# Memory attention and a bilinear FFN on one core: the maximum over tokens is spread by transposition and DRAM transfers, the first w_out block is converted whole, and the engines' orders are written anew

## The chip, the core and the metric

The kernel runs on one core of a Trainium2 chip. A core has five instruction streams: TensorE (PE in the profile; its weight loads are PEld), VectorE (DVE), ScalarE (ACT), GpSimd (POOL) and SyncE (SP), which issues the DMAs. The metric is the time of one execution on the device in microseconds; the runs of the kernel before took 499.88 us in the median.

## The reference, cut to what matters

Eight batches, eight heads, 576 tokens, head dimension 64, 32 memories for each head:

```python
a = phi - np.max(phi, axis=2, keepdims=True)          # over the 576 tokens
a = np.exp(a)
a = a / (np.sum(a, axis=2, keepdims=True) + 1e-09)
k_m = np.einsum('bhsm,bhsd->bhmd', a, k)
v_m = np.einsum('bhsm,bhsd->bhmd', a, v)
scores = matmul(q, k_m^T) / sqrt(64)                  # softmax over the 32 memories
x = softmax(scores) @ v_m                             # -> (4608, 512)
...
a = x @ w1
b = x @ w2
return (a * b @ w3) @ w_out                           # 512x1024, 512x1024, 1024x1024, 1024x512
```

The four weights come as 64-bit words and are turned into fp32 on the chip.

## The kernel before, in words

**What is computed where.** The product w3 @ w_out doesn't depend on the tokens, so the kernel forms it once (`product`, L607) and then needs only one matrix multiplication behind a*b. Its first half (list token W0k, with X for block k = 0) uses w3's columns of one half, the second half (W1k) those of the other; k counts 8 blocks of 128 rows. Each weight block is loaded by SP (`fetch`, L523) and converted in five stages C1 to C5 on ScalarE and VectorE, one stage of one task at a time. Attention works with phi in two layouts: `ph` (memories on the partitions, tokens along the free axis; for the maximum and the sum over tokens) and `a` (tokens on the partitions; for the products with k and v). The maximum is found in `ph` by VectorE (`top`, L212: one value for each of 128 partitions and two halves), but it must be subtracted in `a`, where the memories run along the free axis: every partition needs all 256 values. `spread_max` (token `bm`, L230) makes them with two TensorE transpositions of a broadcast column into a PSUM bank, and `sub_max` (token `bs`, L236 and L240) adds that bank to `a`; `exp_tok` (`be`, L244, ScalarE) follows, then `memories` (`mem`, L252 and L261), which multiplies `a` with the k and v rows (tiles kv0, kv2 and kv4, loaded at L181 and L188, and the chunk in kv2 used first), `blocks` (L283), and `scores` (L301, with `q`). `tokens_down` (L316) turns the scores so that VectorE can do the softmax (L328 to L344).

**The FFN part.** For each batch of 576 tokens the products with the folded weights are done as fp32 pairs of high and low parts (h and l tokens, L497 and L814) in a scheme of seven block products (P{i}{q}, L744, six records each; then O{i}{part}, L829, twelve records each). M tokens (L416) are the products of the next batch's memories with w1 and w2. In the first batch A tokens (L714) stand in for P.

**What sets the order.** Four lists of tokens, written by hand, give the order in which every engine is fed: FIRST for batch 0, SECOND for batch 1, BATCH for batches 2 to 6, LAST for batch 7. An engine takes its instructions strictly in this order. A token without a prefix belongs to the attention of the batch after the one whose FFN is being done, "-" to that batch itself, "+" to the one after next; "!" moves an elementwise step that can run on either engine to GpSimd (for a cast: from ScalarE). phi, tok, kv and q tokens issue loads; SP's queue is in the same order, so a transfer that has to wait holds back all those behind it. The list FIRST also holds the conversion stages. At the start TensorE runs WARM short matmuls (L700).

Of the kernel before, what the change touches and what calls it, by code (L numbers as in the profile page):

```python
# [41 lines left out]
SECOND = """
P10 s00 s01 P11 P20 c10 v10 P60 P50 k200 k201 P70 k502 P30 e202 v20! s10 s11 P21 phi1 c11 tok1 P51 P61 k512 e402 P31
top k210 k211 bm e212 P40 f0! bs kv1 exp -M3 P71 v11 c30 P12 -Mr3 v30 s20 s21 e412 v21! -Ms3 v41! v40! P41 c31 v31 P62
P22 be f3 f2! mem -Mh3 h10 c12 -Ml3 l10! phi2 -Mt3! P52 k220 k221 v12 norm h11 memc P72 +top k522 -Mu3! e422 block
blockc P32 P42 sc0 sc1 +exp e222 f1! scc0 scc1 v42! v22! l11! Sa0 c32 v32 P13 O10 s30 s31 Sa1 mx2 sb2 tok2 h60! P63
k230 k231 +norm P53 P73 k532 e432 kv2 P33 e232 h20 l20! O11 ex2 Sb0! v43! +bm +bs h70 P23 c13 v23! Sa2 p1 Sb2 P43 c33
O20 Sa3! v13 +be Sb1! v33 h61 +mem h21 l60! sm2 M0 Mh0 l21 l61 Sc3! +memc Sb3 l70 O60 Sc2! Mr0 O61 h50 u2 O70 Ms0 Mt0
mu2 h51 O21 C11 l50 O50 h31 tr2 Ml0 l31 Mu0 Sc1! +block l51! O51 h71 l71 +blockc Sc0 M2 h41 q2 ah0 al0 T1! h30 l30 T3!
ah1 p5 M1 Mh1 O71 h40 Mh2 O30 O31 al1 C22 Mr1 T2 Th1! l40 O40 Ms1 Mt1 l41 Mu1! T4 C12 O41 C21 Mr2 Ml1 Tl1 Th0! Tl0!  # L50
Ms2 Mt2! Ml2 Mu2!
"""
# [962 lines left out]
```

## Time and profile before

| what | value |
| --- | --- |
| runs (median of 3) | 499.88 us (499.07 to 500.0) |
| profiled execution's own time | 500.0 us |
| span of its trace | 498.2 us |
| PE busy | 489.3 us, 98% |
| DVE, ACT, POOL busy | 433.3, 340.3, 264.2 us |

The own time is what that execution took as the runs are timed; the span is the stretch that its trace covers, 1.8 us less. Busy times are sums over the engine's instructions; matmuls overlap in their pipeline, so a record of 0.29 us starts 0.13 us after the one before it.

### The profile page before, as it was taken

To read this page: it belongs to the slowest core of one execution; us is meant where nothing else is said; L and a number is where in the kernel's file an instruction comes from. 1 tells how busy PE (TensorE), PEld (TensorE's weight loads), DVE (VectorE), ACT (ScalarE), POOL (GpSimd) and SP (SyncE) were. 2 spreads that over 40 slices of the span, in tenths; PEclk is the share of its full clock that TensorE was granted. 3 is DMA by queue.
4 is the path that set the end of the run, shared out by engine and by line. 5 is a ranking of instruction groups with operands and counts; after the bars stand their busy time and mean duration, and the time that the engine had idled before them with its cause. 6 is when DMAs were issued, how large, how long until landed. Compare 5 with 4: busy or idle time off the path is not lost.

```text
span 498.2 us, 11298 instructions
## 1 busy us (share of the span) xinstructions
PE 489.3 (98%) x4320; PEld 421.3 (85%) x4320; DVE 433.3 (87%) x813; ACT 340.3 (68%) x722; POOL 264.2 (53%) x256
## 2 busy tenths in 40 slices
PE   7898999999999999999999999999999999999997
PEld 6344449888989989989998999899998999899997
DVE  4969899999989998999799979998998878997782
ACT  6877899766777776667576846675757565756651
POOL 0007136673638548844685277716773487447532
PEclk9999999999999999999999999999999999999999
DMA  8999932620476047100830056003800120010002
GB/s 275 413 408 416 420 143 92 282 97 3 126 304 239 3 143 270 64 3 24 296 157 2 25 204 250 1 26 120 333 1 26 61 107 2 25 49 25 2 1 96
DMA packets 22534, 68.89 MB, mean 138 GB/s; under 512 B 1744, under 2 KB 9936, under 8 KB 20432
## 3 DMA queue, kind: packets, MB, share of 16 engines
q1 hardware_dynamic: 22480, 68.16, 36.3%
q8 instruction: 34, 0.56, 0.5%
q14 instruction: 20, 0.16, 0.1%
HBM read 58.72 MB, written 9.44 MB: 137 GB/s over the span
## 4 chain that ended last, share of the span: by engine, by line
PE 91%; DMA 4%; DVE 2%; ACT 1%; issue 1%; SPq 1%; DVEq 0%; ACTq 0%
PE ps L829 36%; PE ps L744 32%; PE ps L416 6%; PE ps L607 6%; PE ps L714 5%; DMA raw<-in_w3T 4%; PE ps L252 3%; PE ps L301 2%; PE ps L261 1%; DVE wo L595 1%; DVE w L595 1%; SPq L523 1%; PE ps L283 0%; ACT w L580 0%; PE ps L230 0%
## 5 line engine op out<-in xcount | busy, mean ns | idle before, releaser
L829 PE MATMUL ps<-sh,Wh 128*128 128x288 f32 x448 | 133.1, 297 | 0.0
L829 PE MATMUL ps<-sl,Wh 128*128 128x288 f32 x448 | 132.1, 295 | 0.1
L829 PE MATMUL ps<-sh,Wl 128*128 128x288 f32 x448 | 132.1, 295 | 0.0
L814 POOL TENSOR_TENSOR sl<-g,sh 128x576 fp32r<-128x576 f32 x42 | 63.4, 1508 | 74.5 <-ACT sh L497 50.4
L829 PEld LDWEIGHTS ps<-sh,Wh 128*128 128x128 f32 x448 | 84.2, 188 | 6.8 <-ACT mh L427 4.2
L829 PEld LDWEIGHTS ps<-sl,Wh 128*128 128x128 f32 x448 | 84.2, 188 | 0.4 <-DVE sl L814 0.4
L829 PEld LDWEIGHTS ps<-sh,Wl 128*128 128x128 f32 x448 | 84.2, 188 | 0.0
L497 ACT CAST sh<-g 128x576 fp32r<-128x576 f32 x81 | 54.8, 685 | 23.5 <-PE ps L829 12.1
L607 PE MATMUL ps<-wo,w 128*128 128x512 f32 (+1 forms) x132 | 56.6, 584 | 3.3 <-DVE w L595 2.0
L769 DVE TENSOR_TENSOR c<-ps,c 128x288 f32<-128x288 f32 x112 | 44.9, 452 | 10.5 <-ACT c L763 8.1
L763 ACT COPY c<-ps 128x288 f32<-128x288 f32 x112 | 41.9, 412 | 16.8 <-PE ps L744 14.9
L607 PEld LDWEIGHTS ps<-wo,w 128*128 128x128 f32 x132 | 24.5, 190 | 33.7 <-issue 27.9
L744 PE MATMUL ps<-sh,ms 128*128 128x288 f32 x224 | 51.2, 295 | 0.0
L724 ACT COPY a_sb<-ps 128x288 f32<-128x288 f32 x72 | 29.6, 411 | 22.0 <-PE ps L744 19.9
L814 DVE TENSOR_TENSOR sl<-g,sh 128x576 fp32r<-128x576 f32 x56 | 42.9, 768 | 0.8 <-ACT sh L497 0.4
L434 DVE TENSOR_TENSOR ml<-ps,mh 128x512 fp32r<-128x512 f32 x64 | 41.0, 682 | 1.8 <-ACT mh L427 1.8
L744 PEld LDWEIGHTS ps<-sh,ms 128*128 128x128 f32 x224 | 38.1, 188 | 1.0 <-ACT ps L757 0.8
L728 DVE TENSOR_TENSOR g<-ps,a_sb 128x288 f32<-128x288 f32 x72 | 32.1, 448 | 5.3 <-ACT a_sb L724 3.9
L427 ACT CAST mh<-ps 128x512 fp32r<-128x512 f32 x64 | 34.6, 598 | 2.7 <-PE ps L416 2.7
L452 DVE TENSOR_TENSOR tmp<-ps,tmp 128x256 f32<-128x256 f32 x84 | 32.8, 418 | 3.4 <-ACT mh L427 2.1
L744 PE MATMUL ps<-ah,mh 128*128 128x288 f32 x112 | 34.7, 310 | 0.0
L744 PE MATMUL ps<-sh,mh 128*128 128x288 f32 x112 | 33.3, 298 | 0.0
(152 smaller groups left out, 1286.8 us busy)
## 6 DMA issues: line engine op xcount, KB each, us to landing
kv<-in_kv SPq DMA_DIRECT2D x16, 1024.0 KB, 8.9
q<-in_qT SPq DMA_DIRECT2D x8, 1152.0 KB, 6.5
outT<-c SPq DMA_DIRECT2D x31, 288.0 KB, 2.2
raw<-in_w3T SPq DMA_DIRECT2D x5, 1024.0 KB, 13.3
ph<-in_phiT SPq DMA_DIRECT2D x8, 576.0 KB, 5.3
a<-in_phi_tok SPq DMA_DIRECT2D x8, 576.0 KB, 5.5
raw<-in_w SPq DMA_DIRECT2D x4, 1024.0 KB, 17.4
kv<-in_w SPq DMA_DIRECT2D x3, 1024.0 KB, 12.7
```

The lines of the kernel that those rows point to most:

```text
L416: nc.tensor.matmul(ps[t][g * M : (g + 1) * M], lhsT=vm[b % 2][d, g], rhs=w12_sb[q][d, :, g], start=True, stop=True,)
L427: nc.scalar.copy(out=mh[:, t], in_=ms["ps", q][t].rearrange("p (w f) -> p w f", w=2))
L434: nc.vector.tensor_tensor(out=ml[:, t], in0=x, in1=ms[q][0][:, t].bitcast(F32), op=ALU.subtract)
L452: nc.vector.tensor_tensor(out=tmp[:, j], in0=x, in1=tmp[:, y], op=op)
L497: nc.scalar.copy(out=out, in_=in_)
L607: nc.tensor.matmul(pw[r][i][0][pw[r][i][1]][:, cols], lhsT=x[:, i * P : (i + 1) * P], rhs=wos[k // half][:, k % half, cols], start=k == 0 ...
L728: engine.tensor_tensor(out=G[n, f // half][:, f % half], in0=b, in1=a, op=ALU.mult)
L744: nc.tensor.matmul(G[bank, q][w][:, :HALF], lhsT=xs[x][:, w], rhs=ys[y], start=i in (1, 5) and k == 0, stop=i in (2, 3, 4) and k == 2, ski ...
L763: nc.scalar.copy(out=G["kept", i, q][:, j], in_=x)
L769: nc.vector.tensor_tensor(out=c, in0=x, in1=c, op=ALU.add)
L814: flexible().tensor_tensor(out=lo, in0=src, in1=hi.bitcast(F32), op=ALU.subtract)
L829: nc.tensor.matmul(ps[j][:, :HALF], lhsT=piece(x, s, 2 * part + k)[:, jc], rhs=y[:, k], start=i in first and part == 0 and k == 0 and t == ...
```

## The change

**The maximum.** A constant tile `maxima` (128 partitions x 32) takes the maxima, the sums and one of the softmax's statistics. The tiles of the pooled keys and values become two halves of one tile `kvm`. A new step `put_max` (token `bn`) transposes `maxima` in 32x32 blocks on VectorE (L231 of the changed kernel) into `kvm`, and two DMAs (L234) write four partitions of 32 values each to DRAM. `spread_max` (`bm`) then broadcasts these 1 KB from DRAM to all partitions by one DMA into `kvm` (L240), and `sub_max` reads it from SBUF. Batches 0 and 1 keep the two TensorE transpositions; batches 2 to 7 take the new way.

**The product of the weights.** The first w_out block is one conversion task in place of two, X has two parts in place of three, and W1k may be done in halves (W1{k}{side}), with PSUM pairs taken for each side. **WARM** goes from 18 to 16. **The lists** are new throughout.

```diff
-WARM = 18
+WARM = 16
...
@@ -118,12 +118,15 @@
     const = ctx.enter_context(tc.tile_pool(name="const", bufs=1))
     att = ctx.enter_context(tc.tile_pool(name="att", bufs=1))
+    dram = ctx.enter_context(tc.tile_pool(name="dram", bufs=1, space=bass.MemoryType.DRAM))
     psum = ctx.enter_context(tc.tile_pool(name="psum", bufs=1, space=bass.MemoryType.PSUM))
     ident = const.tile([P, P], F32, name="ident")
     make_identity(nc, ident)
-    km = [const.tile([P, NG, M], F32, name=f"km{i}") for i in range(2)]
-    vm = [const.tile([P, NG, M], F32, name=f"vm{i}") for i in range(2)]
+    kvm = [const.tile([P, 2, NG, M], F32, name=f"kvm{i}") for i in range(2)]
+    km, vm = [x[:, 0] for x in kvm], [x[:, 1] for x in kvm]
+    maxima = const.tile([P, M], F32, name="maxima")
+    nc.gpsimd.memset(maxima, 0.0)
     NQ = 4
     PLAIN = [(0, 1, 2, 3)] + [()] * (B - 1)
     NA = 4 if PLAIN[1] else 3
@@ -208,11 +211,11 @@
         def top():
             v["ph"] = loaded.pop(("ph", b))
-            v["mx"] = att.tile([P, NT], F32, name="mx")
+            v["mx"] = maxima[:, :NT]
             nc.vector.tensor_reduce(out=v["mx"], in_=v["ph"], axis=AX.X, op=ALU.max, negate=True)
         def exp():
-            v["sm"] = att.tile([P, NT], F32, name="sm")
+            v["sm"] = maxima[:, NT : 2 * NT]
             ph, mx, sm = v["ph"], v["mx"], v["sm"]
             for t in range(NT):
                 nc.scalar.activation(
@@ -223,22 +226,36 @@
             nc.vector.tensor_scalar_add(v["sm"], v["sm"], 1e-9)
             nc.vector.reciprocal(out=v["sm"], in_=v["sm"])
+        def put_max():
+            lines = kvm[b % 2][:, 0, 0]
+            nc.vector.transpose(out=lines, in_=maxima)
+            v["row"] = dram.tile([NT, NG, M], F32, name="row", tag="row", bufs=2)
+            for t in range(NT):
+                nc.sync.dma_start(out=v["row"][t], in_=lines[t :: M])
+
         def spread_max():
-            v["mxb"] = Pair(1, full=False)
-            ps = v["mxb"][0][:, : NT * P]
+            if "row" in v:
+                v["mxb"] = kvm[b % 2].rearrange("p a g m -> p (a g m)")
+                row = v["row"].rearrange("t g m -> (t g m)").unsqueeze(0).broadcast_to([P, NT * P])
+                nc.sync.dma_start(out=v["mxb"], in_=row)
+                return
+            v["bank"] = Pair(1, full=False)
+            v["mxb"] = v["bank"][0][:, : NT * P]
             for t in range(NT):
-                nc.tensor.transpose(ps[:, t * P : (t + 1) * P], v["mx"][:, t : t + 1].broadcast_to([P, P]), ident)
+                x = v["mx"][:, t : t + 1].broadcast_to([P, P])
+                nc.tensor.transpose(v["mxb"][:, t * P : (t + 1) * P], x, ident)
         def sub_max():
-            ps, n = v["mxb"][0][:, : NT * P], NT * P
+            mxb, n = v["mxb"], NT * P
             v["a"] = loaded.pop(("a", b))
             a = v["a"][:, : 4 * n].rearrange("p (c x) -> p c x", c=4)
-            nc.vector.tensor_tensor(out=a, in0=a, in1=ps.unsqueeze(1).broadcast_to([P, 4, n]), op=ALU.add)
+            nc.vector.tensor_tensor(out=a, in0=a, in1=mxb.unsqueeze(1).broadcast_to([P, 4, n]), op=ALU.add)
             for t in range(NT):
                 half = slice(t * D, (t + 1) * D)
                 x = v["a"][half, 4 * n :]
-                nc.vector.tensor_tensor(out=x, in0=x, in1=ps[half, t * P : (t + 1) * P], op=ALU.add)
-            v["mxb"].done()
+                nc.vector.tensor_tensor(out=x, in0=x, in1=mxb[half, t * P : (t + 1) * P], op=ALU.add)
+            if "bank" in v:
+                v["bank"].done()
         def exp_tok():
             nc.scalar.activation(out=v["a"], in_=v["a"], func=AF.Exp)
@@ -320,6 +337,8 @@
             return slice(0, 2) if n == 2 else slice(n, n + 1)
         def stats(n):
+            if n == 1:
+                return maxima[:, 2 * NT : 2 * NT + NBLK].unsqueeze(1).unsqueeze(3)
             x = att.tile([P, 2 - n % 2, NBLK, 1], F32, name="st", tag=f"st{n % 2}")
             return x[:, both(n)] if n == 0 else x
-                 "bm": spread_max, "mem": memories, "block": blocks}
+                 "bn": put_max, "bm": spread_max, "mem": memories, "block": blocks}
         parts = {"sc": scores, "scc": tokens_down, "mx": soft_max, "sb": soft_sub, "ex": soft_exp, "sm": soft_sum,
                  "mu": soft_mul, "tr": probs, "ah": probs_high, "al": probs_low, "Th": sums_high, "Tl": sums_low}
...
-    groups = [[("w30", 0, 1, QUARTER[0]), ("wo", 0, 1, QUARTER[0]), ("wo", 0, 1, QUARTER[1]), ("w30", 0, 1, QUARTER[1])]]
+    groups = [[("w30", 0, 1, QUARTER[0]), ("wo", 0, 1, slice(0, DF // 2)), ("w30", 0, 1, QUARTER[1])]]
...
@@ -540,7 +559,7 @@
         def word():
             if "u" not in v:
-                if i % 2:
+                if (i + len(tasks)) % 2:
                     u = const.tile([P, CW], I32, name="uw", tag="Wl3")
                 elif g < LATE:
                     u = init.tile([P, CW], I32, name="u")
-        if k == 0 and r not in pw:
-            pairs = [Pair(), Pair()]
-            pw[r] = [(pairs[i // 2], i % 2) for i in range(4)]
+        for half_of in sorted({i // 2 for i in rows_of}):
+            if (r, half_of) not in pw:
+                pw[r, half_of] = Pair()
-                pw[r][i][0][pw[r][i][1]][:, cols],
+                pw[r, i // 2][i % 2][:, cols],
...
-            pair, j = pw[step != "K"][i]
+            pair, j = pw[int(step != "K"), i // 2], i % 2
-                    product(0, 0, *((range(2), QUARTER[0]), (range(2), QUARTER[1]), (range(2, 4),))[x])
+                    product(0, 0, range(2 * x, 2 * x + 2))
-                    product(*digits)
+                    r, k, *side = digits
+                    product(r, k, *(range(2 * i, 2 * i + 2) for i in side))
```

One line of BATCH, before and now:

```diff
-phi2 P10 -M3 s00 s01 P20 c10 v10 P60 k200 k201 P50 P70 k502 P30 e402 v40! e202 -Mr3 -Ms3 v20! P11 P40 s10 s11 c30 v30
...
+P10 s00 s01 -M3 P20 P60 k200 k201 P50 P70 c10 v10 k502 P30 e402 P11 P40 -Mr3 e202 v20! s10 s11 P61 c30 -Ms3 v30 -Mh3
```

TensorE in the first stage, up to the first scores. Before (`ident, mx` are batch 0's transpositions of the maxima, L252 and L261 its memories, L283 its blocks, L301 its scores; `w` and `wo` are the blocks of w3 and w_out, and rows with `x8` at L607 are two blocks k):

```order
L607 MATMUL ps<-wo_82,w_250 128x512 x8
L230 MATMUL ps<-ident,mx 128x128 x2
L607 MATMUL ps<-wo_81,w_278 128x512 x8
L252 MATMUL ps<-kv_262,a 32x128 x8
...
L261 MATMUL ps<-kv_264,a 32x128 x8
L283 MATMUL ps<-ident,kvm 128x128 x2
L301 MATMUL ps<-q,km_71 32x288 x16
L607 MATMUL ps<-wo_81,w_297 128x512 x8
```

Now, where L626 is the product, L269 and L278 the memories, L300 the blocks and L318 the scores:

```order
L626 MATMUL ps<-wo_84,w_265 128x512 x8
L246 MATMUL ps<-ident,maxima 128x128 x2
L626 MATMUL ps<-wo_83,w_278 128x512 x6
L269 MATMUL ps<-kv_248,a 32x128 x8
...
L278 MATMUL ps<-kv_250,a 32x128 x8
L626 MATMUL ps<-wo_83,w_297 128x512 x2
L300 MATMUL ps<-ident,kvm 128x128 x2
L626 MATMUL ps<-wo_83,w_278 128x512 x2
L318 MATMUL ps<-q,kvm_73 32x288 x16
L626 MATMUL ps<-wo_83,w_297 128x512 x6
```

Ten matmuls of w3's second half stand ahead of the scores in place of eight, four of them between memories and scores.

SyncE's queue in one batch of the list BATCH. Before (`ph` and `a` are the two layouts of phi, `kv` k and v, `outT` results):

```order
L841 DMA outT<-c 128x2x288
L168 DMA ph<-in_phiT 128x1152
L173 DMA a<-in_phi_tok 128x1152
L181 DMA kv_3307<-in_kv 128x2x1024
L181 DMA kv_3309<-in_kv 128x2x1024
L188 DMA kv_3311<-in_kv 128x512
L841 DMA outT<-c 128x2x288 x3
```

Now (`row` is the DRAM tile of the maxima):

```order
L860 DMA outT<-c 128x2x288 x2
L176 DMA a<-in_phi_tok 128x1152
L171 DMA ph<-in_phiT 128x1152
L234 DMA row<-kvm_74 4x32 x2
L240 DMA kvm_74<-row 128x256
L184 DMA kv_3358<-in_kv 128x2x1024
L184 DMA kv_3360<-in_kv 128x2x1024
L191 DMA kv_3362<-in_kv 128x512
```

Three transfers of the maxima now stand ahead of the loads of k and v, and `ph` comes behind `a`.

VectorE in the same batch, around the subtraction of the maximum. Before (L212 is the maximum, L236 and L240 the subtraction, L316 the transposition of the scores, L328 and L332 the softmax's maximum and its subtraction, L728 and L769 parts of the FFN):

```order
L212 TENSOR_REDUCE mx<-ph 128x2
L434 TENSOR_TENSOR ml<-ps,mh 128x512 x2
L769 TENSOR_TENSOR c<-ps,c 128x288 x4
L728 TENSOR_TENSOR g_3086<-ps,a_sb 128x288
L236 TENSOR_TENSOR a<-a,ps 128x1024
L240 TENSOR_TENSOR a<-a,ps 64x128 x2
L728 TENSOR_TENSOR g_3086<-ps,a_sb 128x288
L728 TENSOR_TENSOR g_3088<-c 128x288
L316 STREAM_TRANSPOSE s_sb<-ps 128x288 x4
```

Now (L215 the maximum, L231 the new transposition, L252 and L256 the subtraction, L333, L347 and L351 the softmax, L747 and L788 the FFN):

```order
L215 TENSOR_REDUCE maxima<-ph 128x2
L788 TENSOR_TENSOR c<-ps,c 128x288 x4
L747 TENSOR_TENSOR g_3069<-ps,a_sb 128x288
L231 STREAM_TRANSPOSE kvm_74<-maxima 128x32
...
L333 STREAM_TRANSPOSE s_sb<-ps 128x288 x4
L347 TENSOR_REDUCE st<-s_sb 128x36
...
L788 TENSOR_TENSOR c<-ps,c 128x288 x4
L351 TENSOR_TENSOR s_sb<-s_sb,st 128x1152
L747 TENSOR_TENSOR g_3072<-c 128x288
L252 TENSOR_TENSOR a<-a,kvm_74 128x1024
L256 TENSOR_TENSOR a<-a,kvm_74 64x128 x2
```

The subtraction stood ahead of the softmax's transposition and stands now behind the softmax's own subtraction.

## Rows read from the trace of the kernel before

**Rows 1.** Page, busy time of each engine, its share of the span, and instructions.

```profile
PE 489.3 (98%) x4320; PEld 421.3 (85%) x4320; DVE 433.3 (87%) x813; ACT 340.3 (68%) x722; POOL 264.2 (53%) x256
```

**Rows 2.** Waits of PE: line, what it waited for; us in total, times, longest.

```profile
PE ps L607 <- DVE w L595: 2.0, 2, 1.3
```

**Rows 3.** Chain that ended last, in order of time: start us, us, what.

```profile
128.73 0.68 DVE sl L814
...
132.63 8.80 PE ps L744 x66
...
242.12 1.02 PE ps L416 x16
...
252.86 0.22 PE ps L230 x2
...
256.67 9.73 PE ps L744 x72
...
266.40 1.88 PE ps L252 x64
```

**Rows 4.** Windows: us, then busy (count) of PE, PEld, DVE, ACT, POOL, granted clock, DMA.

```profile
51.46:129.31 77.85, 77.85 (x629) 58.54 (x614) 75.41 (x130) 63.49 (x107) 37.14 (x37) 1.00 0.42 161
241.33:293.89 52.56, 52.56 (x518) 48.40 (x518) 47.27 (x91) 35.04 (x84) 31.77 (x31) 1.00 0.31 110
```

**Rows 5.** Timeline of PE, 10 to 52 us: start, us, what, in brackets the wait before.

```profile
13.96 24.45 PE L607 MATMUL ps<-wo,w 128*128 128x512 f32 x56 [1.28 <-DVE wo L595]
...
50.21 1.66 PE L301 MATMUL ps<-q,km 64*32 64x288 f32 x32 [0.36 <-ACT km L289]
```

**Rows 6.** Line L193, 20 to 60 us: the load of batch 0's q.

```profile
L193 SPq DMA_DIRECT2D q<-in_qT x1: 2462/2462/2462, 31.1 to 31.1; - x1
...
DMA to landing us min/median/max: 17.6/17.6/17.6
```

**Rows 7.** Timeline of DVE at the first transposition of scores and at one Q subtraction.

```profile
51.46 1.58 DVE L316 STREAM_TRANSPOSE s_sb<-ps 128x288 f32<-128x288 f32 x4 [2.39 <-PE ps L301]
...
96.68 1.22 DVE L940 TENSOR_TENSOR w<-w 64x1024 f32<-64x1024 f32 x1
```

**Rows 8.** Lines L168 (133 to 136 us) and L181 (134 to 138 us): SECOND's first loads.

```profile
L168 SPq DMA_DIRECT2D ph<-in_phiT x1: 487/487/487, 134.0 to 134.0; - x1
...
DMA to landing us min/median/max: 4.5/4.5/4.5
...
L181 SPq DMA_DIRECT2D kv<-in_kv x2: 422/444/466, 135.8 to 136.3; - x2
...
DMA to landing us min/median/max: 8.2/9.3/10.3
```

**Rows 9.** Timeline of DVE in the batch that starts at 241.33 us.

```profile
249.38 1.34 DVE L212 TENSOR_REDUCE mx<-ph 128x2 f32<-128x1152 f32 x1
...
253.71 1.21 DVE L236 TENSOR_TENSOR a<-a,ps 128x1024 f32<-128x1024 f32 x1
254.84 0.58 DVE L240 TENSOR_TENSOR a<-a,ps 64x128 f32<-64x128 f32 x2
...
255.82 0.45 DVE L728 TENSOR_TENSOR g<-c 128x288 f32<-128x288 f32 x1
...
259.84 1.54 DVE L769 TENSOR_TENSOR c<-ps,c 128x288 f32<-128x288 f32 x4
...
262.16 1.35 DVE L332 TENSOR_TENSOR s_sb<-s_sb,st 128x1152 f32<-128x1152 f32 x1
```

**Rows 10.** Timeline of ACT in the same batch: the exponential over tokens.

```profile
259.41 1.18 ACT L244 ACTIVATE a<-a 128x1152 f32<-128x1152 f32 x1
```

**Rows 11.** Page, DMA issues: a half result; count, KB each, us from issue to landing.

```profile
outT<-c SPq DMA_DIRECT2D x2, 144.0 KB, 1.8
```

**Rows 12.** Line L523, 69 to 71 us: one load of 1 MB that had the queues to itself.

```profile
DMA to landing us min/median/max: 4.7/4.7/4.7
```

**Rows 13.** Line L814 on DVE: duration ns min/median/max, first and last start.

```profile
L814 DVE TENSOR_TENSOR sl<-g,sh x56: 694/751/1227, 97.9 to 489.7; 128x576 fp32r<-128x576 f32 x56
```

More of the change, by code (lines that the diff above doesn't have):

```diff
@@ L41 @@
 """
 SECOND = """
[L43 to L51, printed above, removed]
+P11 s10 phi1 tok1 s11 P10 P21 P61 s00 s01 c11 v11 P20 c10 v10 P60 k200 k201 P50 k502 top bn exp k210 k211 P12 P70 e402
+v40 P30 e202 v20! P40 c30 v30 P51 k512 P71 e412 h10 P31 e212 P41 bm kv1 norm v21 s20 bs s21 -M3 -Mh3 P22 c12 c31 l10
@@ new lines @@
+phi2 -Mr3 P62 k220 v12 k221 -Ml3 f1 be P52 -Ms3 -Mt3 v31 k522 P72 e422 h11 +top mem memc tok2 +bn v41! P32 e222 block
+blockc f3! P13 sc0 +exp scc0 sc1 scc1 -Mu3! P42 O10 c32 v32 mx2 v42! s30 s31 P23 c13 v13 +bm +bs P53 h20 P63 l11! sb2
+l20 k230 k532 k231 O11 p1 P73 +be e432 v43 v22! +norm P33 f0 P43 c33 Sa0 v33 Sa1 Sb0 Sc1 Sa3 e232 f2! v23 O20 kv2 +mem
+h21 l21 Sc3! h60 ex2 M0 +memc Sa2! h61 Sb1! O21 l60 O60 Sc2! l61 h50 l50 sm2 +block C11 mu2 O61 tr2 h70 Sb3 h71 Sb2 u2
+l70! h51 l51! O50 l71 Mh0 O70 +blockc Mr0 ah0 h40 Sc0! h30 Ms0 Mt0 O51 h41 Ml0 q2 O71 M2 M1 l30 p5 O30 C22 al0! Mh2
@@ L52 @@
+Mu0 Mr1 ah1! l40 T1 Ms1 h31! l31 al1 Mh1 T3! O40 l41 Mt1 T2 T4 O31 Mu1 Th1 Th0 C12 Ml1 Tl0! Tl1! Mr2 Ms2 Mt2! Mu2! O41
+C21 Ml2
 """
 BATCH = """
-phi2 P10 -M3 s00 s01 P20 c10 v10 P60 k200 k201 P50 P70 k502 P30 e402 v40! e202 -Mr3 -Ms3 v20! P11 P40 s10 s11 c30 v30
-h10! -Mh3 P61 k210 k211 P51 +top -Ml3 -Mt3! P21 k512 P31 c11 e212 +exp -Mu3! P71 +bm P12 e412 P41 f0 v11 s20 s21 c31
-P62 sc1 tok2 +bs l10! v31 sc0 v41 kv2 scc0 scc1 k220 h11! P22 P52 v21! c12 v12 mx2 P13 k522 k221 P32 e222 f3 P72 s30
@@ new lines @@
+tok2 P51 k512 -Ml3 P21 P31 v40! phi2 +top k210 k211 e212 P71 e412 -Mt3! -Mu3! f0 c11 v11 P12 s20 s21 +bn P41 c31 v31
+v21! h10! P22 sc0 +exp sc1 v41! P62 k220 scc0 k221 scc1 P52 P72 +bm P13 h11 l10! c12 k522 mx2 f3 v12 e422 P32 s30 s31
+P23 f2 c13 e222 kv2 P63 k230 k231 sb2 f1 ex2 P53 v42 k532 +bs +be l11! v22 Sa0 P73 P42 Sb0 e432 v43! c32 v32 h20 +norm
+P33 e232 v23! Sa1! v13 sm2 P43 +mem M0 +memc M1 l20! Mh0 c33 v33 M2 Sa2 Ml0 Sa3 h21 Mr0 Ms0 Sb3 O10 O11 p1 Sc1! Sb1!
+h50 Mt0 l21 Sc2! O20 O21 Sb2! h60 l50 Mu0 C11 l60 O50 h61 Mh2 h51 O60 l61 O61 Sc0 mu2 l51! O51 tr2 h71 Sc3! h70 Mh1
@@ L62 @@
+l70 l71 ah0 Mr1 u2 O70 h30 al0 p5 l30! O71 h40 l40! Ml1 ah1 h31 Ms1 al1! l31 +block +blockc C22 T1 T3 h41 l41 Mt1 Mu1
+O30 O31 q2 T2 Th1! Mr2 T4 Tl1! O40 C12 O41 C21 Th0 Tl0! Ms2 Mt2! Mu2! Ml2
 """
 LAST = """
-Mr1 P10 s00 s01 P11 +bm P20 P60 k200 Ml1 k201 P50 P70 c10 v10 k502 e402 P30 e202 Mr0 T1 +be P40 c30 v20! -M3 v40 s10
-s11 P61 v30 h10 -Mh3 -Ml3 phi2 f0 sb2 l10! ah0 P51 k210 kv2 k211 P71 k512 e412 -Mr3 M2 Mu0! -Ms3 -Mt3 P31 e212 P21 tr2
-sc1 Mt0 P12 s20 s21 scc1 Ms2 Mh0 v41! v21 P41 c31 v31 Mt2! +block f3! al1 q2 P22 c12 v12 P52 k522 +blockc c11 -Mu3!
```

48 lines of the change are left out of this document (23 added, 25 removed).

## The prediction, as put on record before the changed kernel ran

> **What bounds the kernel now.** I read the busy times first. TensorE is busy for 489.3 us of a span of 498.2 [rows 1], so there are 8.9 us in which it does nothing, and all else that can be won must come from work taken off it. The waits of TensorE come next: the largest group is 2.0 us, for the conversion of w3 in the first stage [rows 2], and behind the first scores the engine waits hardly at all. The chain of waits says the same in order of time: block products, memories and output units of TensorE stand in it back to back. The one step of another engine behind the first stage is VectorE's low part at 128.73 us, 0.68 us long, ahead of the end of the first list at 132.63 [rows 3]. The windows show why it is there. Between 51.46 and 129.31 us TensorE is busy for all of the 77.85 us, but VectorE is busy for 75.41 of them: in FIRST both engines are full, and the end of that list is held by whichever is later. In a batch of BATCH, TensorE is busy for 52.56 of 52.56 us and VectorE for 47.27; there only TensorE counts, at a granted clock of 1.00 [rows 4]. So the change is read at three places: up to the first scores, FIRST from there to its end, and the batches behind.
>
> **The transpositions removed.** In six of eight batches two transpositions go from TensorE's order. A pair takes 0.22 us of the chain [rows 3]: 6 x 0.22 = 1.32 us less, certain as long as TensorE is the bound of those batches. VectorE gets one 128x32 transposition for each; four of 128x288 take 1.58 us, 0.40 each [rows 7], so it is under 0.4, and I take 0.15. The subtraction keeps its size: from PSUM 1.21 us [rows 9], and 64x1024 from two SBUF tiles 1.22 us [rows 7].
>
> **The first stage.** The scores need q, and q needs the DMA queues, full till then: issued at 31.1 us, it lands 17.6 later, at 48.7 [rows 6]. Scores started at 50.21 after a short wait for ScalarE [rows 5], and TensorE waited for converted weights before that. The change moves the memories ahead and puts loads in another order, but as many bytes precede q, so I keep 48.7 as a floor. Memories, blocks and the copies between them lie ahead of it in my count, so scores start at about 49.0, and VectorE's first transposition comes at about 50.2 in place of 51.46 [rows 7]: 1.3 earlier. The whole w_out block, the half products and two warming matmuls fewer cost nothing here, since conversion ahead of q's landing covers them. If that cover were gone, the whole block would be ready later than its first quarter, and the price is at most one wait like that of 1.28 us before [rows 5].
>
> TensorE has done more by then: 42 full-width matmuls of the weights' product, before 40 in full-width terms. One matmul is two records of 24.45 / 56 = 0.44 us [rows 5], so 2 x 2 x 0.44 = 1.75 us of work are done ahead. With the scores 1.2 us earlier TensorE alone would end FIRST 2.9 to 3.1 us sooner.
>
> **The rest of FIRST.** VectorE has 134 instructions from its first transposition to the last low part, 129 before. By rows they are 2.4 to 2.7 us more: one Q subtraction of 64x1024, 1.22 [rows 7]; five of 288 columns, 1.54 / 4 = 0.39 each [rows 9]; less one low part of 0.75 [rows 13]. Its share was 75.41 of 77.85 us [rows 4], so it has no more than 2.4 us of slack, and new lists would have to use all of it. Against that the last low part now stands one output unit nearer to TensorE's end, 12 records of 0.135 (9.73 / 72, [rows 3]) = 1.6 us. So by VectorE: -1.3 + 2.5 - 1.6 = -0.4, and I take **-0.5 us** for FIRST. The bounds are TensorE's -3.1, if VectorE's gaps take the extra work, and +1.0, if none of the 1.6 is kept and half the earlier start goes.
>
> **SECOND: k and v behind the maximum.** SP's queue now has three small transfers ahead of k and v. One instruction waiting there holds back kv0, kv2, kv4 and what follows. Measured from FIRST's end: phi was issued 1.4 us after it and landed 4.5 later [rows 8], at +5.8. The maximum takes 1.34 [rows 9], the transposition 0.15: rows are issued at +7.3. No row shows a transfer of 0.5 KB; the nearest is a half result of 144 KB, 1.8 us [rows 11], and it can't be under the issue itself, 0.4 [rows 8]. I take 2.0, as it also waits for a semaphore on either side (range 1.0 to 3.0). Then the broadcast is issued and k and v behind it, from +9.7 on. A lone load of 1 MB lands in 4.7 us [rows 12]; before, kv2 landed 2.6 us after kv0 (136.3 + 10.3 against 135.8 + 8.2, [rows 8]). So kv2, which the memories use first, lands at 9.7 + 4.7 + 2.6 = +17.0, or +17.4 with the broadcast's own issue of 0.4 ahead; I take +17.25 (16.2 to 18.4 by the range of the small transfers). TensorE comes to the memories after 19 block products (114 x 0.135) and one M step of 1.02 [rows 3], at +16.4. That is a wait of **+0.9** (0 to 2.0). The scores of that batch now follow after 12 records of cover, 1.6 us, for the copies and blocks between; I put **+0.1** on it (0 to 0.5). The list's second use, for batch 3, has phi issued behind these loads, landed at about +18.7, rows at +20.2 and kv2 9.7 later at +29.9; its memories are due nine products, three output units and the other attention (some 3.9 us) later, at 16.4 + 7.3 + 4.9 + 3.9 = +32.5, so nothing is put on it (0 to 1).
>
> **BATCH, four uses.** A batch's rows are issued behind P71, at 13 x 0.81 + 1.02 = 11.6 us, plus VectorE's queue of some 1.8: +13.4. kv2 lands 2.4 + 4.7 + 2.6 later, at 23.1 to 23.3. The memories stood at 266.40 - 241.33 = 25.07 [rows 3, 4] and come 0.22 earlier: 24.85. So these loads are hidden with 1.5 us to spare. The subtraction is another matter. It stood at 253.71, 12.7 us ahead of the memories; it now comes behind the softmax's. From the end of P32 VectorE and ScalarE have in a row: two c of 0.39, the softmax's subtraction 1.35, one g 0.45, the subtraction 1.21 + 0.58 [rows 9], the exponential 1.18 [rows 10]: 5.54 us. TensorE has seven block products, 42 x 0.135 = 5.67. The margin is 0.1, before what passes between engines; I take a wait of **0.1** a batch, four times: **+0.4** (0 to 2.4). Who waits behind the memories is everything, as TensorE is strictly in order.
>
> Here the row on contention matters. A low part, two SBUF inputs of 576 columns, took 694 to 1227 ns with a median of 751 [rows 13], so the same instruction can lose up to 0.5 us. The subtraction before had one input in PSUM; now it has both in SBUF while GpSimd is busy 31.77 of 52.56 us [rows 4]. The Trainium skill, "SBUF — State Buffer", section "Who interferes with whom", says that a VectorE instruction with two SBUF inputs contends with a GpSimd instruction that reads SBUF, and that such a hold is a full block rather than a slowing. The spread of [rows 13] agrees with it. By that rule the subtraction would be the instruction that loses, and the sum that of the slower rival below; by the median row it loses nothing.
>
> The Trainium skill, "DMA: Bandwidth & Descriptors", section "Anatomy of one DMA — SWDGE (gpsimd) path", gives about 2.0 us as a fixed cost of a transfer on that path; no row here shows one so small, and the sum above goes by the 1.8 us row.
>
> **The sum.** The profiled execution took 500.0 us of its own time (span 498.2 and 1.8 around it), 0.12 above the median of the runs, 499.88. -1.32 - 0.5 + 0.9 + 0.1 + 0.4 = -0.42: 499.58, less 0.12 for the median is 499.46. I predict **499.5 us**. A change under 0.2%, 1.0 us, can't be told from none by this measurement.
>
> **The rivals.**
> *TensorE's lead survives FIRST.* For it: in the window of FIRST, VectorE's gaps are 2.44 us, as much as the added work, and more steps were given to GpSimd, busy for only 37.14 of 77.85 us [rows 4]. Against it: the low part in the chain at 128.73 [rows 3]. Then FIRST gives -2.6 in place of -0.5: 497.4. Chance 0.27.
> *All new waits are hidden.* Small transfers take 1.0 and not 2.0, and the margin of 0.1 holds: 500.0 - 1.32 - 0.5 - 0.12 = 498.1. Chance 0.08.
> *The maximum's chain is late (the other side).* The path from the maximum to `a` is VectorE, DMA, DMA, VectorE, ScalarE in place of two short transpositions. If the subtraction loses 0.5 to 0.7 us beside GpSimd, as the slowest of [rows 13] did, its whole delay falls on the memories, since the margin is 0.1: 4 x 0.6 = 2.4 more, and 1.0 more in SECOND, at the upper bound for the small transfers: 499.5 + 2.4 + 1.0 = 502.9. It decides for slower from a wait of about 0.45 us a batch on. For it: the margin and [rows 13]; against it: the median there, 751 ns. Chance 0.22.
> That the change doesn't do what it says is excluded for the transpositions, which are gone from TensorE's order.
>
> **How the numbers follow.** The forecast's own case has 0.43 and lies between 498.9 and 500.9. The rivals to the fast side hold 0.35, the one to the slow side 0.22. The range is 497.2 to 501.8. Its low end takes in the first rival at 497.4, but not the case that TensorE keeps the whole 3.1 us; its high end to 0.45 us more a batch and 0.5 more in SECOND, midway to the slower rival. Some 0.1 are left out on each side. Faster by over 0.2% is the sum of the first two rivals, 0.35; within 0.2% 0.43; slower 0.22.
>
> **What would show it.** Right: TensorE's record of the memories in SECOND begins about 17 us after FIRST's end, with a wait of near 1 us for kv, and each batch takes 52.4 to 52.5 us; FIRST ends at 131.9 to 132.3 with a low or high part ahead of its last units. Wrong: FIRST's end at or under 130 us; waits of 0.5 us and more ahead of the memories in each batch, for `a`; a subtraction above 1.6 us; row transfers that take over 3 us; or scores of batch 0 that start at 50 or later.

## The result, and the profile after

The changed kernel took 502.5 us in the median of six runs (501.6 to 503.77), the kernel before 499.66: ratio 1.0059, 95% interval 1.0047 to 1.0070. It is 0.6% slower, where no change to speak of was forecast, and lies 0.7 us above the range. The profiled execution took 503.25 us of its own time, 3.25 more than that of before.

The page's busy times stand against [rows 1]: TensorE has more busy time with fewer instructions.

```profile
PE 492.1 (98%) x4300; PEld 422.6 (84%) x4300; DVE 421.2 (84%) x802; ACT 341.6 (68%) x725; POOL 261.5 (52%) x266
```

The timeline of TensorE gives the ends of the lists, by the first block product (high part of the attention times high part of the folded weights) behind the last output unit. Before, in the second and third list:

```profile
132.46 0.29 PE L744 MATMUL ps<-ah,mh 128*128 128x288 f32 x1
...
188.59 0.29 PE L744 MATMUL ps<-ah,mh 128*128 128x288 f32 x1
```

In the changed kernel:

```profile
129.76 0.30 PE L763 MATMUL ps<-ah,mh 128*128 128x288 f32 x1
...
190.39 0.30 PE L763 MATMUL ps<-ah,mh 128*128 128x288 f32 x1
```

FIRST ends 2.70 us earlier; SECOND takes 60.63 us for 56.13, 4.50 more. The windows of the changed kernel (columns as in [rows 4]) give FIRST from its first A product on, SECOND's memories, and one batch:

```profile
70.75:129.76 59.01, 58.76 (x558) 52.29 (x557) 56.77 (x105) 45.25 (x89) 31.30 (x31) 1.00 0.34 126
...
148.90:152.44 3.54, 3.54 (x72) 3.26 (x79) 2.39 (x4) 1.15 (x3) 3.48 (x3) 0.53 0.08 31
296.08:348.74 52.66, 52.66 (x517) 48.44 (x516) 45.57 (x89) 35.86 (x84) 32.07 (x32) 1.00 0.34 117
```

In the first row TensorE is busy for 58.76 of 59.01 us, and its chain ends FIRST without VectorE's low part, which stood in that of before [rows 3]:

```profile
120.13 9.81 PE ps L848 x72
```

So TensorE, not VectorE, sets FIRST's end now. In the second the granted clock is 0.53: the memories ran at half clock, 1.2 GHz, and took 3.54 us where [rows 3] has 1.88. The third is a batch without any wait, and yet 0.10 us longer than before's 52.56 [rows 4], though two transpositions have left it.

The waits of TensorE, against [rows 2]:

```profile
PE ps L626 <- DVE wo L614: 2.0, 2, 1.2
PE ps L269 <- ACT ms L516: 1.7, 1, 1.7
...
PE ps L763 <- DVE g L747: 0.4, 1, 0.4
```

The second and third are new, and both lie in SECOND. The chain there, from phi's load to the memories (L269):

```profile
130.87 3.96 DMA ph<-in_phiT
...
134.85 1.36 DVE maxima L215
...
136.24 0.22 DVE kvm L231
...
137.16 1.52 DMA row<-kvm
...
138.77 3.81 DMA kvm<-row
...
142.82 1.22 DVE a L252
...
148.90 3.54 PE ps L269 x64
```

The order is what matters: maximum, transposition, rows (1.52 us), broadcast (3.81 us), subtraction. SP issues k and v directly behind the broadcast, and phi for the batch after next behind them:

```profile
136.48 1.17 SPq L234 DMA_DIRECT2D row<-kvm  x2
138.77 0.33 SPq L240 DMA_DIRECT2D kvm<-row  x1
139.14 0.95 SPq L184 DMA_DIRECT2D kv<-in_kv  x2
140.53 0.34 SPq L191 DMA_DIRECT2D kv<-in_kv  x1
140.98 0.44 SPq L171 DMA_DIRECT2D ph<-in_phiT  x1
```

### The profile page after: what moved, and what is told of

Read it like the earlier page. It is cut to its first block, busy times and chain, and to the rows that moved or that the text cites. A ratio compares the mean times of both kernels' runs of the same rounds, so it can differ in the third digit from the quotient of the medians.

```text
span 501.5 us, 11267 instructions
## 1 busy us (share of the span) xinstructions
PE 492.1 (98%) x4300; PEld 422.6 (84%) x4300; DVE 421.2 (84%) x802; ACT 341.6 (68%) x725; POOL 261.5 (52%) x266
## 4 chain that ended last, share of the span: by engine, by line
PE 92%; DMA 3%; DVE 2%; ACT 1%; SPq 1%; issue 0%; DVEq 0%
PE ps L848 36%; PE ps L763 28%; PE ps L626 11%; PE ps L435 6%; PE ps L733 5%; PE ps L269 3%; PE ps L318 2%; DMA raw<-in_w_out 1%; DMA ph<-in_phiT 1%; DMA kvm<-row 1%; PE ps L278 1%; SPq L542 0%; ACT ph L221 0%; PE ps L300 0%; DMA row<-kvm 0%
## 5 line engine op out<-in xcount | busy, mean ns | idle before, releaser
L833 POOL TENSOR_TENSOR sl<-g,sh 128x576 fp32r<-128x576 f32 x40 | 59.0, 1480 | 64.8 <-ACT sh L516 64.7
L516 ACT CAST sh<-g 128x576 fp32r<-128x576 f32 x87 | 58.9, 688 | 18.4 <-PE ps L848 10.3
L626 PE MATMUL ps<-wo,w 128*128 128x512 f32 x128 | 57.0, 598 | 2.0 <-DVE wo L614 2.0
L782 ACT COPY c<-ps 128x288 f32<-128x288 f32 x112 | 40.8, 407 | 22.1 <-PE ps L763 20.8
L788 DVE TENSOR_TENSOR c<-ps,c 128x288 f32<-128x288 f32 x112 | 45.5, 452 | 11.5 <-ACT c L782 7.3
L747 DVE TENSOR_TENSOR g<-ps,a_sb 128x288 f32<-128x288 f32 x72 | 32.5, 453 | 25.5 <-ACT a_sb L743 24.5
L626 PEld LDWEIGHTS ps<-wo,w 128*128 128x128 f32 x128 | 23.6, 190 | 32.3 <-issue 27.7
L833 DVE TENSOR_TENSOR sl<-g,sh 128x576 fp32r<-128x576 f32 x58 | 46.1, 803 | 5.6 <-POOL sh L514 4.7
L747 POOL TENSOR_TENSOR g<-c 128x288 f32<-128x288 f32 x41 | 34.1, 837 | 14.4 <-DVE c L788 14.4
L776 ACT COPY ps<-ps 128x288 f32<-128x288 f32 x56 | 20.4, 384 | 21.2 <-PE ps L763 18.3
```

The lines of the kernel that those rows point to most:

```text
L516: nc.scalar.copy(out=out, in_=in_)
L626: nc.tensor.matmul(pw[r, i // 2][i % 2][:, cols], lhsT=x[:, i * P : (i + 1) * P], rhs=wos[k // half][:, k % half, cols], start=k == 0 and ...
L747: engine.tensor_tensor(out=G[n, f // half][:, f % half], in0=b, in1=a, op=ALU.mult)
L782: nc.scalar.copy(out=G["kept", i, q][:, j], in_=x)
L788: nc.vector.tensor_tensor(out=c, in0=x, in1=c, op=ALU.add)
L833: flexible().tensor_tensor(out=lo, in0=src, in1=hi.bitcast(F32), op=ALU.subtract)
```

## The experiments

All are compared with the kernel before, timed on the same chip in the same group (499.3 to 499.6 us in the median); the groups ran on different chips, so differences between groups are taken from each group's own kernel before. The table has the stretches of each run's profiled execution, from rows like those above: FIRST's end, SECOND's length, and a batch of BATCH.

| kernel | us, median | FIRST ends | SECOND | a batch |
| --- | --- | --- | --- | --- |
| before | 499.66 | 132.46 | 56.13 | 52.56 |
| changed | 502.5 | 129.76 | 60.63 | 52.66 to 52.85 |
| after_again | 502.48 | 130.05 | 59.07 | 52.65, one 53.05 |
| first_only | 499.76 | 129.54 | 57.11 | 52.79 to 52.89 |
| kv_early | 504.96 | 129.31 | 62.79 | 52.70 |
| old_second | 498.62 | 129.64 | 57.11 | 52.70, one 53.31 |
| before_pad32 | 499.70 | 131.80 | 56.13 | 52.63 |
| before_m32 | 502.2 | 131.31 | 56.81 | 52.85 |
| after_pad32 | 500.11 | 129.12 | 59.18 | 52.45 |
| after_pad64 | 501.61 | 129.23 | 61.72 | 52.51 |
| first_only_pad32 | 497.68 | 129.15 | 57.02 | 52.58 |
| nb_S1_pad32 | 499.77 | 129.46 | 59.23 | 52.44 |
| kv2_first_pad32 | 500.1 | 129.10 | 60.55 | 52.43, one 53.13 |
| old_second_pad32 | 496.35 | 129.25 | 56.78 | 52.45 |
| old_second_bn_pad32 | 507.61 | 129.66 | 65.73 | 52.43 |

**after_again**: the changed kernel, unchanged. 

> The changed kernel once more, beside the others of its group. In its trace three stretches differ from before: the first list ends 2.70 us earlier, the second takes 60.63 us for 56.13, and each of the following batches 52.65 to 52.85 for 52.56, though two transpositions less (0.22) stand in it. Theory: these are properties of the kernel, so they come again: 502.5 us (501.5 to 503.8), second list 58.5 to 60.7, batches 52.6 to 52.9, with intervals of 133 to 134 ns from one 288-column matmul to the next (132.3 before). Rival: the slower matmuls belong to that one execution; then the batches take 52.3 to 52.4 and the whole 501 or less.

It came again: ratio 1.006 (1.0047 to 1.0073). This execution kept the full clock in SECOND, and its list of waits names another releaser than the first one's:

```profile
PE ps L269 <- DMA kv<-in_kv: 1.5, 2, 1.2
...
PE ps L763 <- DVE g L747: 1.0, 1, 1.0
```

So the wait ahead of the memories is for k and v, not for ScalarE's cast: here the memories began at 149.31, and that cast (L516) ran until 149.75. In the first trace it only happened to end last. Of the 1.5 us, 1.2 lie in SECOND and the rest in the one batch of 53.05: the loads are late in BATCH too, at times. Its chain shows both, in SECOND and in that batch:

```profile
139.96 9.21 DMA kv<-in_kv
...
149.31 1.95 PE ps L269 x64
...
310.31 9.42 DMA kv<-in_kv
...
319.87 1.95 PE ps L269 x64
```

**first_only**: the three lists behind FIRST are those of before.

```diff
 SECOND = """
-P11 s10 phi1 tok1 s11 P10 P21 P61 s00 s01 c11 v11 P20 c10 v10 P60 k200 k201 P50 k502 top bn exp k210 k211 P12 P70 e402
+P10 s00 s01 P11 P20 c10 v10 P60 P50 k200 k201 P70 k502 P30 e202 v20! s10 s11 P21 phi1 c11 tok1 P51 P61 k512 e402 P31
...
```

> The changed kernel with the lists SECOND, BATCH and LAST of the kernel before, so that the maximum is spread by TensorE in every batch; only the first list and the conversion are new. Theory: TensorE's lead of the first stage survives (2.7 us) and nothing is given back: 497.0 us (496.6 to 497.6), first list ending at 129.8 to 130.0. Rival, the step of the prediction: VectorE holds the end of the first list, 499.3, and what was seen was one execution's. Second rival: what the first list puts off lands in the second, which then takes over 57 us: 498.5 to 499.5.

The theory fell. The first list gained its 2.9 us, but SECOND took 57.11, as the second rival had it, and the whole is 499.76, ratio 1.0004 (0.9995 to 1.0013). With the very lists of before, each batch is 0.23 to 0.33 us longer. The chain shows a stretch of 156 output-unit matmuls in one batch; before, such a row read 20.82 or 20.83 us:

```profile
216.80 20.97 PE ps L848 x156
```

Nothing waits in it. That left the tiles' addresses: the pool of constants has grown by 128 bytes a partition (the 128x32 tile), and the attention's pool has lost three small tiles of 160 bytes in all, so ah, al and the FFN's sh, sl, g, c and a_sb lie 32 bytes lower.

**kv_early**: in SECOND the k and v loads go ahead of the transposition.

```diff
-k502 top bn exp
+k502 kv1 top bn exp
...
-P41 bm kv1 norm
+P41 bm norm
```

> In the list SECOND the loads of k and v for batch 2 (kv1) are issued ahead of the maximum's transposition and its transfers instead of behind the broadcast; nothing else differs from the changed kernel. Theory: TensorE waited ahead of the memories for the second k and v tile, and the half clock behind it came of that wait; with the tile landed some 4 us earlier the wait of 1.7 us, the 0.4 before it in part, and the 1.7 to 1.9 us at half clock go: second list 56.0 to 57.5, whole 499.0 us (498.2 to 500.0). Rival, which the list of waits names: the wait is for ScalarE (cast of the sums) or the maximum's chain; then the wait stays at 1.5 or more and the whole at 502 or above.

The theory fell: 504.96, slower by 2.5 than the changed kernel. k and v were in time now, but the rows stood behind 2.25 MB in the DMA queues and took 5.37 us in the chain, and VectorE stood still ahead of the subtraction (L252), with g, which TensorE needed, queued behind it:

```profile
136.78 5.37 DMA row<-kvm
```

```profile
145.79 1.23 DVE L252 TENSOR_TENSOR a<-a,kvm 128x1024 f32<-128x1024 f32 x1 [3.65 <-issue]
```

```profile
PE ps L763 <- DVE g L747: 3.8, 1, 3.8
```

So there are two users of the same queues, and in SECOND each was late when the other went first.

**old_second**: only SECOND is that of before; the DRAM way stays in BATCH. 

> The changed kernel with the list SECOND of before; FIRST, BATCH and LAST are the new ones, so four of the six uses of the DRAM way stay. Theory: SECOND is where the loss is; it takes 56.1 to 56.6 us again, the whole is 498.0 us (497.5 to 499.0), 0.3 to 1.2 above the kernel that has only the first list new, by the batches' slower matmuls. Rival: the DRAM way itself costs in each batch what it did in the second list; then 500 or more. Second rival, the sum of the prediction: four batches of 0.22 less and 0.1 more each: 0.5 below the kernel that has only the first list new.

498.62, ratio 0.9984 (0.9975 to 0.9993): SECOND is the place of the loss, and the rest, slow matmuls included, is a little faster than before. It is 1.1 us under first_only, not above it as the theory had it: the new BATCH and LAST win, as in the second rival.

**before_pad32**, **after_pad32**, **first_only_pad32**: 32 unused bytes in the attention's pool.

```diff
         t = att.tile([P, NG, S], F32, name="q", tag="q")
+        if b == 0:
+            nc.gpsimd.memset(att.tile([P, 8], F32, name="pad"), 0.0)
```

> The kernel before with one unused tile of 32 bytes a partition added ahead of the attention's high and low parts, so that these, the FFN's tiles sh, sl, g, c and a_sb behind them lie 32 bytes further: at 32 past a multiple of 64 bytes, where the changed kernel has them (before: at a multiple of 64). Theory: matmuls whose moving operand lies so are issued 1 to 2 ns later each, which is what made the batches of all kernels built on the change 0.25 to 0.35 us longer; then this kernel has intervals of 133.2 ns in place of 132.3, batches of 52.8 and is 501.5 us (500.8 to 502.2), 2 slower. Rival: the address doesn't matter, the slower intervals come of the order in which banks are taken or of the chip; then 499.5 as the kernel before.

> The changed kernel with the same unused 32 bytes, which bring ah, al, sh, sl, g, c and a_sb back to a multiple of 64 bytes. Theory: intervals of 132.3 ns, batches 52.35 (two transpositions less than before's 52.56), second list still 58.5 to 60.5 because of its waits: 500.4 us (499.8 to 501.4). Rival: no change, 502.5.

> Only the first list and the conversion new, the lists behind as before, and 32 unused bytes. Theory: the first list ends 2.9 us earlier as in the unpadded kernel and nothing is given back behind it: second list 56.2 to 56.7, batches 52.56, whole 497.3 us (496.8 to 497.9). Rival: 499.8 as without the bytes; then the 2.9 us are lost elsewhere.

Two of three times came as expected, though first_only_pad32's SECOND took 57.02 and not 56.2 to 56.7. The changed kernel goes from 502.48 to 500.11 (499.03 to 502.26), which is 2.9 and 0.8 us above the kernel before of its group, and first_only from 499.76 to 497.68, 0.2 above and 1.6 under; the row of 156 matmuls is back at 20.82, and one of 120 at 16.08 (16.32 and 16.18 in the changed kernel):

```profile
216.28 20.82 PE ps L850 x156
```

```profile
218.26 16.08 PE ps L850 x120
```

The kernel before, moved 32 bytes up, is at 499.70, ratio 1.0008 (1.0000 to 1.0017), not at 501.5. A rule by multiples of 64 bytes was wrong.

**before_m32**, **after_pad64**: the other direction, and twice the distance. In before_m32 the two 8-byte tiles become one, and no order changes:

```diff
-            v["mx"] = att.tile([P, NT], F32, name="mx")
+            v["both"] = att.tile([P, 2 * NT], F32, name="mx")
+            v["mx"] = v["both"][:, :NT]
...
-            v["sm"] = att.tile([P, NT], F32, name="sm")
+            v["sm"] = v["both"][:, NT:]
```

> The kernel before with its two 8-byte tiles of maxima and sums in one tile, which moves the attention's high and low parts and the FFN's tiles 32 bytes down, to the very addresses that they have in the changed kernel (sl at 201632 for 201664); orders and lists are those of before. The kernel with 32 bytes more (sl at 201696) was hardly slower, so a rule by multiples of 64 fell. Theory: it is these addresses themselves, 32 past a multiple of 128, that make the matmuls slow: intervals of 133.2 ns, batches of 52.8, whole 501.3 us (500.6 to 502.0). Rival: it is their place relative to the constant tiles (the folded weights, which lie 128 bytes further in the changed kernel); then intervals of 132.3 to 132.6 and 499.3 to 499.8.

> The changed kernel with 64 unused bytes in place of the 32: sl at 201696, as in the kernel before with 32 bytes more. Theory (32 past a multiple of 128 is slow, 96 is not): intervals of 132.4 to 132.6 ns, batches 52.5 to 52.6, 500.4 us (499.5 to 501.5). Rival (any odd multiple of 32 is slow beside these constant tiles): 133.2 ns, batches 52.65 to 52.85, 502.4.

The kernel before at the changed kernel's addresses is as slow as the changed kernel: 502.2, a little over the forecast's upper bound, ratio 1.0051 (1.0039 to 1.0063), every batch 52.85, with no wait in any of them:

```profile
218.33 21.00 PE ps L830 x156
271.16 21.00 PE ps L830 x156
```

after_pad64 has batches of 52.51 as the theory says; its 501.61 is above the forecast because SECOND took 61.72 in that trace, with waits of 2.1 and 1.1 us and 3.4 us at half clock. So against addresses 64 past a multiple of 128 bytes, those 32 past cost 0.2 to 0.4 us a batch and those 96 past under 0.1, with both sets of constants' addresses. These are three places of the tiles (sl at 201632, 201664 and 201696); that the rule goes by multiples of 128 no run tests, nor which of the moved tiles counts, nor why the chip does so.

**nb_S1_pad32**: bn taken out of SECOND's first use, so that TensorE's transpositions come back there (32 bytes added). 

> The changed kernel with the 32 bytes, and in the list SECOND the first use of the DRAM way (batch 2) taken back: the maximum is spread by two TensorE transpositions, so k and v wait for no transfer. Theory: the wait of TensorE ahead of the memories, the one ahead of it for VectorE's g that stood behind the subtraction, and the half clock all come of that one use; second list 56.0 to 56.8, whole 497.2 us (496.7 to 498.0), 3 less than with it. Rival: the second list is slow by its order of the other work, and stays at 58 or more; whole 499.5 or above.

The rival held, but for a reason of its own:

```profile
PE ps L437 <- DVE a L258: 2.0, 1, 2.0
```

The new order has no PSUM bank to spare at that place: the M products (L437) wait until the subtraction (L258) has read the spread maxima. The way through SBUF frees that bank, and the new order uses it. The run can't price the DRAM way.

**kv2_first_pad32**: kv2 and kv4 ahead of kv0 (32 bytes added).

```diff
-bm kv1 norm
+bm kvx1 kvy1 norm
```

> The changed kernel with the 32 bytes; in SECOND the tile of k and v that the memories use first (kv2) and the short one (kv4) are issued ahead of kv0, at the same place behind the broadcast. Theory: the wait of 1.3 us ahead of the memories is for kv2's landing; issued first it lands some 2.5 us earlier, the wait goes or falls to 0.3 and with it any half clock; the wait of 1.2 us for g, behind the subtraction that waits for the broadcast, stays or grows by 0.2: second list 57.8 to 58.3 in place of 59.2, whole 498.9 us (498.3 to 499.6). Rival: the wait moves to kv0, used second, or to the broadcast, and nothing is won: 499.8 to 500.4.

The rival held: the memories began at 147.10, 1.6 us earlier than in after_pad32 (148.71), and then waited in their midst for the other tile:

```profile
147.10 0.64 PE L271 MATMUL ps<-kv,a 128*32 128x128 f32 x16
149.21 1.52 PE L271 MATMUL ps<-kv,a 128*32 128x128 f32 x48 [1.46 <-DMA kv<-in_kv]
```

All of k and v is late, not one tile of it.

**old_second_pad32**: SECOND of before and the 32 bytes. 

> The changed kernel with the 32 bytes and the list SECOND of before: the DRAM way only in the four uses of BATCH. Theory, from the stretches measured one by one: first list ends 2.9 to 3.3 earlier, second list 57.0 (0.9 more), four batches of 52.45 (0.11 less each) and the last 0.3 less: 499.3 - 3.2 + 0.9 - 0.45 - 0.3 = 496.3 us (495.8 to 496.9), the fastest of all. Rival: without the second list's work moved ahead, what BATCH expects is late and a wait comes in its first batch: 497.5 or more.

496.35 (496.18 to 496.5), ratio 0.9938 (0.9926 to 0.9949): the fastest, as the sum of the measured stretches had it. Apart from FIRST's, one wait of half a microsecond is left, behind FIRST's end:

```profile
PE ps L765 <- POOL sl L412: 0.5, 1, 0.5
```

**old_second_bn_pad32**: the same with the DRAM way in SECOND's old order.

```diff
-P31 top k210
+P31 top bn k210
...
-P72 +top k522
+P72 +top +bn k522
```

> The fastest kernel so far (496.35 us: first list, BATCH and LAST new, SECOND of before, 32 unused bytes) with the DRAM way put into SECOND's old order: the transposition and the row transfers directly behind each maximum, the broadcast where the TensorE transpositions stood, k and v behind it as they were behind the subtraction's token. Theory: the way through DRAM costs in SECOND in any order, since it starts only when phi has landed, 5 us into the list, and needs some 12 us up to the exponential's end, with the memories due at 15.4: two waits of TensorE, 2 to 3.5 us in all, 498.8 us (497.8 to 500.0). Rival: it was the new order, with the memories and VectorE's work drawn together, that had no room; then 496.0 to 496.8.

507.61, ratio 1.0166 (1.0142 to 1.0190): more than the theory's upper bound. SECOND takes 65.73 us, 8.95 more than with TensorE's transpositions in that order. VectorE waits 5.12 us ahead of the subtraction, TensorE as long for the g behind it, and 6.8 us at half clock follow:

```profile
PE ps L765 <- DVE g L749: 5.1, 1, 5.1
PE ps L271 <- ACT a L263: 1.7, 1, 1.7
```

So the new order didn't make the price of the DRAM way in SECOND but reduced it: with it SECOND takes 59.18 us (after_pad32), against 56.78 with the old order and the transpositions. That no order of SECOND could take the DRAM way without a loss isn't shown; these are the only two tried with it.

## Why the prediction was wrong, by its own steps

**FIRST, forecast -0.5: mis-sized, -2.70.** The step "by VectorE", -1.3 + 2.5 - 1.6, failed. TensorE's lead of the first stage survived, as the first rival had it: scores began at 48.60, without a wait, and the first A product 3.43 us earlier than before (70.75 for 74.18). From VectorE's first transposition to the end of its last low part, before and now (columns as in [rows 4]):

```profile
51.46:129.39 77.93, 77.85 (x629) 58.54 (x614) 75.49 (x130) 63.57 (x108) 37.14 (x37) 1.00 0.42 160
49.41:127.04 77.63, 77.38 (x628) 58.07 (x613) 75.04 (x135) 64.48 (x108) 35.95 (x38) 1.00 0.43 167
```

So the three terms came out as -2.05, -0.30 and -0.35. The five added instructions took 2.7 us, as priced, but the others, of the same shapes, took 2.4 us less in sum than before, so VectorE's busy time fell where 2.5 us more were forecast. Its idle time hardly changed (2.4 and 2.6 us). The softmax's subtraction shows a part of it; in before, GpSimd ran all through the one of 1376 ns:

```profile
L332 DVE TENSOR_TENSOR s_sb<-s_sb,st x4: 751/758/1376, 53.7 to 111.5; 128x576 f32<-128x576 f32 x4
L351 DVE TENSOR_TENSOR s_sb<-s_sb,st x2: 750/751/752, 52.2 to 106.1; 128x576 f32<-128x576 f32 x2
```

Part of the -2.70 may be the traced execution of before: the kernel before with its tiles moved ended FIRST at 131.80 and 131.31, not at 132.46. And 0.9 us of the gain come back in SECOND even with its old list (57.02 for 56.13); 0.7 of them are a wait for GpSimd's low part (first_only_pad32):

```profile
PE ps L765 <- POOL sl L412: 0.7, 1, 0.7
```

**SECOND, forecast +1.0 and -0.44 for two pairs: +4.50 in the profiled execution, +2.9 in the second.** The rows were priced nearly right (1.52 us in the chain and 2.29 from the first one's issue to the broadcast's, forecast with their semaphores 2.0). (The Trainium skill, "DMA: Bandwidth & Descriptors", section "Anatomy of one DMA — SWDGE (gpsimd) path", has some 2.0 us as the fixed cost on another path; these took 1.52 from SP.) The broadcast was priced as an issue only: that its landing holds VectorE's subtraction, and g behind it in VectorE's strict order, was not followed, though the wait it adds was named for SP. It took 3.81 us with k and v issued behind it at 0.4 us: the subtraction began 4.04 us after the broadcast's issue here, and 2.94 in kv_early, where k and v had gone ahead. kv2 was due at 17.25 us behind FIRST's end (the 17.4 above the sum of 17.0 counts the broadcast's issue twice), and the memories began at 19.1 (148.90 - 129.76) and, in after_again, 19.3. The issues were on time (the broadcast's at +9.0, forecast +9.3); kv2 itself took 9.21 us in after_again, where the sum had 4.7 + 2.6 = 7.3. A load that had the queues to itself was the wrong row to size it by: [rows 8] had up to 10.3 for these loads, and two loads of 1 MB at 4.7 each make 9.4, an estimate from [rows 12]. What part the broadcast and phi have in it no run separates. And the wait carried a second price: in the profiled execution the clock fell to half behind TensorE's waits of 0.4 and 1.7 us, 1.7 us more for the memories alone (3.54 for 1.88). The kernel before had no such wait behind FIRST and no half clock until its end.

**BATCH, forecast -0.22 and +0.1 each, -0.12 together: -0.11 each at the old addresses.** Batches of 52.58 with the old lists (first_only_pad32) became 52.45 with the new ones. The sum was right, but the 0.1 came elsewhere: no ordinary batch waits for `a` ahead of its memories, and about 1 us earlier block products start 0.20 and 0.24 us apart in place of 0.13, in each of these batches (old_second_pad32):

```profile
314.81 0.29 PE L765 MATMUL ps<-ah,ms 128*128 128x288 f32 x1
315.01 0.40 PE L765 MATMUL ps<-sh,mh 128*128 128x288 f32 x1
315.25 0.29 PE L765 MATMUL ps<-sl,mh 128*128 128x288 f32 x1
```

What holds them no run here shows. The margin for k and v, "1.5 us to spare", was wrong for the reason above: in single batches of three traces TensorE waited 0.3 to 0.6 us for them.

**Addresses: a term that was missing.** Against the kernel before of its group, the changed kernel loses 2.1 us less with 32 bytes (2.9 and 0.8), first_only 1.9 less, and the kernel before loses 2.9 by the opposite shift. Nothing in the diff says so but the sizes of small tiles.

**Together**, each step against the kernel before of its group and with the other lists held: FIRST alone 497.68 - 499.32 = -1.6; BATCH and LAST, the further step to 496.35 - 499.34 = -3.0, are -1.35; SECOND, from there to 500.11 - 499.32 = +0.8, is +3.8; addresses, from there to 502.48 - 499.55 = +2.9, are +2.1. The steps follow one another, so that they add up to +2.9 is no test of them; another order of steps could share it out otherwise.

**The slower rival's time, 502.9, was near by luck.** Its mechanism, a subtraction that loses beside GpSimd, never came about. It took 1216 to 1224 ns in all six uses with both inputs in SBUF, 1212 to 1220 with one in PSUM (the line's two forms in the changed kernel):

```profile
L252 DVE TENSOR_TENSOR a<-a,kvm x6: 1216/1218/1224, 142.8 to 370.2; 128x1024 f32<-128x1024 f32 x6
L252 DVE TENSOR_TENSOR a<-a,ps x2: 1212/1216/1220, 37.4 to 87.3; 128x1024 f32<-128x1024 f32 x2
```

But that is no test of the rival, for in the windows of these six, added up, GpSimd (POOL) does nothing:

```profile
sum 7.32, PE 7.32 PEld 7.06 DVE 7.32 ACT 6.27 POOL 0.00; mean PE 1.22 PEld 1.18 DVE 1.22 ACT 1.05 POOL 0.00
```

The Trainium skill, "SBUF — State Buffer", section "Who interferes with whom", lets a VectorE instruction with two SBUF inputs contend with a GpSimd instruction that reads SBUF; these six can't show it either way. One subtraction of old_second_bn_pad32 did run beside GpSimd and took 1325 ns, where the other five of that kernel took 1219 to 1224:

```profile
168.12 1.32 DVE L254 TENSOR_TENSOR a<-a,kvm 128x1024 f32<-128x1024 f32 x1 [0.43 <-DMA kvm<-row]
167.34 2.78 POOL L749 TENSOR_TENSOR g<-c 128x288 f32<-128x288 f32 x2
```

## What to carry to other kernels

A detour through DRAM is not priced by its bytes: it stands in the queues with the large loads around it, and here each made the other late when it was issued first, so look at what is issued within a few microseconds on either side and at who is queued behind the instruction that waits for it. Price a wait of TensorE with the half clock that may follow it, when the engine had none before. Don't take the times of VectorE's instructions as fixed when a list moves them: here the same shapes took 2.4 us less in FIRST. And when a change adds or drops small tiles, look where the large ones have moved: here 32 bytes were worth 1.9 to 2.9 us of 500, and keeping the new first list, the new BATCH and LAST, the old SECOND and the old addresses gave 496.35 us.
